# Attention's key and query projections as fp32 products, one head in each half of TensorE's rows, in steps of three token tiles

## The chip, the core and the metric

One NeuronCore of a Trainium2 chip runs the whole program. The metric is device time in microseconds (us) of one execution, the median over runs. PE is TensorE; its weight loads are listed as an engine of their own, PEld. DVE is VectorE, ACT is ScalarE, POOL is GpSimd, and SP issues most of the DMAs.

## What is computed

Linear attention over 4 batches, 8 heads, 576 tokens and a head dimension of 64, then two mixture-of-experts stages over the 2304 tokens. Only the attention is changed:

```python
def phi(x):
    proj = np.einsum('bhsd,df->bhsf', x, w_phi)          # 64 -> 128 features
    proj = proj - np.max(np.abs(proj), axis=-1, keepdims=True)
    return np.concatenate([np.exp(proj), np.exp(-proj)], axis=-1)
q_p, k_p = (phi(q), phi(k))
kv = np.einsum('bhsf,bhsd->bhfd', k_p, v)
z = np.sum(k_p, axis=2)
num = np.einsum('bhsf,bhfd->bhsd', q_p, kv)
den = np.einsum('bhsf,bhf->bhs', q_p, z)[..., None] + 1e-06
return (num / den).astype(np.float32)
```

## The kernel before

Attention runs over eight units; a unit is two batches by two heads, and has nine tiles (j) of 128 tokens with the two heads side by side (64 + 64 columns). For keys and for queries each tile goes through the same chain. A PE transpose (L115, tile `pt`) puts the 128 columns on the partitions, head 0 on rows 0 to 63 and head 1 on rows 64 to 127. ACT copies it out of PSUM rounded to fp32r (`kh`, `qh`, L76), and DVE takes the rounding error (`kl`, `ql`, L79). `proj` (L122) multiplies by a block-diagonal weight that holds `w_phi` twice, rounded (`wbh`) and its error (`wbl`): three fp32r matmuls of 256 columns a tile (L126 to L128) give the features of both heads. `center` (DVE, L133 and L135) subtracts the row's largest absolute value, and `expo` (ACT, L144 and L145) makes exp of both signs, `f`.

From the keys' `f`, `kv_mm` (L180) accumulates the state of both heads over the tiles of a batch. The fifth tile (j = 4) holds 64 tokens of each of the two batches, so its products read rows 0 to 63 for batch 0 and rows 64 to 127 for batch 1. ACT copies the finished state out (`kvt`, L184), `augment` (L193) multiplies it by a constant and ACT copies that to `kvf`. The queries' `f` are transposed (`q_tr`, L212, `ptq`), copied to `fq` (L215), multiplied by `kvf` (`num`, L224, `pn`), copied to `nT` (L225), transposed back (`finish`, L235, `po`) and divided on DVE.

The loop over `g` walks steps of two tiles (one in the last of a unit's five), keys one unit ahead of queries. A step projects its tiles, takes the exponentials of the step before and uses those of the step before that; `fillers` puts `num`, `augment`, `finish` and the next units' transposes between. A scheduler then orders each engine's instructions when the program is built, and each engine runs its own list in that order. After unit 3 the router of the first half of the tokens (`Router.route`) runs on DVE, with a few small matmuls (`pr`, L444 to L453) in PE's list. PSUM has eight banks, which here are two each for the tags T (transposes), Pj (projections), K (the state, one head a bank) and N (the rest). The mixture stages follow, and start while attention ends.

An fp32 product is two matmuls in the trace, with a weight load each, where the program lists one; a transpose and an fp32r product are one.

Of the kernel before, what the change touches and what calls it, by code (L numbers as in the profile page):

```python
# [7 lines left out]
F32 = mybir.dt.float32  # L8
# [30 lines left out]
def attention(tc, nc, cp, q, k, v, w_phi, w_gate, w_skip, lgs, routed, stepped, keys_done, last_steps):  # L39
# [3 lines left out]
    with ExitStack() as ctx:  # L43
# [4 lines left out]
        ps = ctx.enter_context(tc.tile_pool(name="psA", bufs=2, space=PSUM))  # L48

        ident = cp["ident"]  # L50
        ws = c1.tile([P, FH], F32, name="ws")
# [3 lines left out]
        wbh = c1.tile([P, 2 * FH], F32R, name="wbh")  # L55
        wbl = c1.tile([P, 2 * FH], F32R, name="wbl")
        with tc.high_priority():
            for t in (wbh, wbl):
                nc.vector.memset(f32(t), 0.0)
        for h in range(2):  # L60
            w, wh, wl = [t[64 * h : 64 * h + 64] for t in (ws, wbh, wbl)]
            sl = slice(h * FH, h * FH + FH)
            nc.vector.tensor_copy(wh[:, sl], w)
            nc.vector.tensor_tensor(wl[:, sl], w, f32(wh)[:, sl], ALU.subtract)
# [7 lines left out]
        lall = c1.tile([P, NJ, H, 9], F32, name="lall")  # L72

        def split(dst_h, dst_l, src, eng_h="act", lo=None):
            if eng_h == "act":
                nc.scalar.activation(dst_h, src, AF.Copy)  # L76
            else:
                nc.vector.tensor_copy(dst_h, src)
            (lo or nc.vector).tensor_tensor(dst_l, src, f32(dst_h), ALU.subtract)  # L79

        def load_q(bp, hp):
            t = wk.tile([P, NJ, 2, DH], F32, name="qt", tag="qt", bufs=1)
            for b in range(2):
                for h in range(2):
                    (nc.sync if bp or hp else nc.scalar).dma_start(
                        t[64 * b : 64 * b + 64, :, h],
                        q[2 * bp + b, 2 * hp + h].rearrange("(p j) d -> p j d", j=NJ),
                    )
            return t

        def load_kv(src, bp, hp, nm):
            if nm == "vt":
                t = kp.tile([P, NJ, 2, 66], F32, name=nm, tag=nm, bufs=3)
                nc.gpsimd.memset(t[:, :, :, 64:66], 1.0)
            else:
                t = kp.tile([P, NJ, 2, DH], F32, name=nm, tag=nm, bufs=1)
# [10 lines left out]
        def transp(t, nm):  # L107
            pool = kp if nm == "k" else wk
            th = pool.tile([P, NJ, P], F32R, name=nm + "h", tag="Th", bufs=2)
            tl = pool.tile([P, NJ, P], F32R, name=nm + "l", tag="Tl", bufs=2)  # L110

            def group(j0, n):
                pt = ps.tile([P, 4, P], F32, name="pt", tag="T")
                for i in range(n):
                    nc.tensor.transpose(  # L115
                        pt[:, i], t[:, j0 + i].rearrange("p h d -> p (h d)"), ident
                    )
                split(th[:, j0 : j0 + n], tl[:, j0 : j0 + n], pt[:, :n])

            return th, tl, [lambda a=a: group(*a) for a in ((0, 4), (4, 4), (8, 1))]  # L120

        def proj(th, tl, j0, n):  # L122
            pp = ps.tile([P, 2, 2, FH], F32, name="pp", tag="Pj")
            for i in range(n):
# [6 lines left out]
        def center(pp, n):  # L131
            m = wk.tile([P, 2, 2], F32, name="m", tag="m", bufs=4)
            nc.vector.tensor_reduce(m[:, :n], pp[:, :n], AX.X, ALU.max, apply_absolute_value=True)  # L133
            t = wk.tile([P, 2, 2, FH], F32, name="t", tag="t", bufs=2)
            nc.vector.tensor_tensor(  # L135
                t[:, :n], pp[:, :n], m[:, :n].unsqueeze(3).to_broadcast([P, n, 2, FH]), ALU.subtract
            )
            return t

        def expo(t, n, nm):  # L140
            f = (kp if nm == "k" else wk).tile([P, 2, 2, 2, FH], F32, name="f", tag="f", bufs=2)
            tf = t[:, :n].rearrange("p n h f -> p (n h) f")
            ff = f[:, :n].rearrange("p n h s f -> p (n h) s f")
# [4 lines left out]
        units = [(bp, hp) for bp in range(2) for hp in range(4)]  # L148
        QS = ((0, 2), (2, 2), (4, 1), (5, 2), (7, 2))
        KS = ((0, 2), (2, 2), (4, 2), (6, 2), (8, 1))  # L150
        st = {}

        def load(nm, u):
            if u < len(units):
                bp, hp = units[u]
                st[nm, u] = load_q(bp, hp) if nm == "qt" else load_kv(k if nm == "kt" else v, bp, hp, nm)

        def prep_v(u):

            st["v", u] = st.pop(("vt", u))  # L160
            load("vt", u + 1)
            st["kv", u] = wk.tile([P, 2, 2, 2, 74], F32, name="kvf", tag="kvf", bufs=2)

        def kv_mm(u, step):
            vt = st["v", u]
            j0, n = KS[step]
            f = st.pop(("f", u, step))
            for i in range(n):
                j = j0 + i
                for b in (0, 1):  # L170
# [3 lines left out]
                    first, last = (j == 0, j == 4) if b == 0 else (j == 4, j == 8)  # L174
                    for h in range(2):
                        if first:
                            st["acc", h] = ps.tile([65, 256], F32, name="kv", tag="K")
                        acc = st["acc", h]
                        r = f[pr, i, h].rearrange("p s f -> p (s f)")
                        nc.tensor.matmul(acc, vt[pr, j, h, 0:65], r, start=first, stop=last)  # L180
                    if last:
                        kvt = kp.tile([65, 2, 256], F32, name="kvt", tag="kvt")
                        for h in range(2):
# [3 lines left out]
        def augment(u, b):  # L187
            kvt = st.pop(("kvt", u, b))
            hp = units[u][1]
            pa = ps.tile([P, 2, 2, P], F32, name="pa", tag="N")  # L190
# [11 lines left out]
        def q_tr(u, step, f, i):  # L202
            j0, n = QS[step]
            if j0 in (0, 5) and i == 0:
                nj = 5 if j0 == 0 else 4
                st["fq"] = st["fq", u, 0 if j0 == 0 else 5] = wk.tile(
                    [P, 2, 2, 2, nj * 64], F32, name="fq", tag=f"fq{nj}", bufs=2
                )
            pt = ps.tile([P, 4, P], F32, name="ptq", tag="T")
            for h in range(2):  # L210
                for sg in range(2):
                    nc.tensor.transpose(pt[:, 2 * h + sg], f[:, i, h, sg], ident)  # L212
            jj = 64 * ((j0 + i) % 5)
            o = st["fq"][:, :, :, :, jj : jj + 64].rearrange("p h s b t -> p (h s) b t")
            nc.scalar.activation(o, pt.rearrange("p g (b t) -> p g b t", b=2), AF.Copy)  # L215

        def num(u, jc, h, b):
            nj = 5 if jc == 0 else 4
            fq, kvf = st["fq", u, jc], st["kv", u]
            if ("nT", u) not in st:  # L220
                st["nT", u] = wk.tile([74, 2, NJ, 2, 64], F32, name="nT", tag="nT", bufs=1)
# [3 lines left out]
            nc.scalar.activation(  # L225
                st["nT", u][:, h, jc : jc + nj, b], pn.rearrange("f (j t) -> f j t", t=64), AF.Copy
            )

        def finish(u, g):
            bp, hp = units[u]  # L230
            nT = st["nT", u]
            po = ps.tile([P, 2, 3, 74], F32, name="po", tag="N")
            for h in range(2):
                for i in range(3):
                    nc.tensor.transpose(  # L235
                        po[:, h, i], nT[:, h, 3 * g + i].rearrange("f b t -> f (b t)"), ident[0:74, 0:74]
                    )
            rd = wk.tile([P, 2, 3, 1], F32, name="rd", tag="rd", bufs=4)
            nc.vector.tensor_scalar(rd, po[:, :, :, 64:65], 1e-6, None, ALU.add)
            nc.vector.reciprocal(rd, rd)  # L240
            if ("x", bp) not in st:
# [3 lines left out]
                x[:, 3 * g : 3 * g + 3, hp * P : hp * P + P].rearrange("p j (h d) -> p h j d", h=2),  # L245
                po[:, :, :, 0:64],
                rd.to_broadcast([P, 2, 3, 64]),
# [3 lines left out]
                lall[:, 3 * g : 3 * g + 3, 2 * hp : 2 * hp + 2, :].rearrange("p j h e -> p h j e"),  # L251
                po[:, :, :, 65:74],
                rd.to_broadcast([P, 2, 3, 9]),
                ALU.mult,
            )
            if g == 2:
# [4 lines left out]
                routed(bp, x, hp, lg, lambda: ps.tile([P, 512], F32, name="pr", tag="N"))  # L261

        NU = len(units)

        def fillers(u, step):
# [1023 lines left out]
```

## Time and profile before

| | before |
|---|---|
| median of 3 runs (lowest to highest) | 2062.34 us (2060.51 to 2065.01) |
| the profiled execution, and its span | 2056.73 us, 2055.0 us |
| PE busy, of the span | 2017.1 us, 98% |
| DVE, ACT, POOL busy | 62%, 46%, 16% |
| granted clock of PE, mean | 0.998 |

A matmul's end is modelled, and matmuls overlap in the records, so a busy PE may still issue faster or slower: the time that one takes from the next is read from start to start. In a row of the timeline, that is the next PE row's start less this row's start, over the row's count.

### The profile page before, as it was taken

The numbers are of one execution on the slowest core, as the hardware profiler recorded it, in microseconds if no ns is written. First come the engines' busy times: TensorE is split into PE (matmuls) and PEld (weight loads), VectorE is DVE, ScalarE is ACT, GpSimd is POOL, SyncE is SP. The second block draws the span as 40 slices with busy tenths as digits, with TensorE's granted clock in tenths as the row PEclk, the third lists the DMA queues.
The fourth block names the chain that finished last, engine by engine and source line by source line (L and its number), as shares of the span: only waits on it lengthen the run. The fifth ranks groups of instructions, "written<-read, shape, count | busy, mean of one in ns | idle before, by whom it ended". The sixth has DMA issues, their size and how long they took to land.

```text
span 2055.0 us, 29087 instructions
## 1 busy us (share of the span) xinstructions
PE 2017.1 (98%) x10815; PEld 1769.5 (86%) x10815; DVE 1269.2 (62%) x2236; ACT 935.4 (46%) x1885; POOL 337.4 (16%) x271
## 2 busy tenths in 40 slices
PE   8999999998999999999999999999999999999999
PEld 6777778997688998988888899989988898998997
DVE  6456476775586666665745666656565666666563
ACT  5766655554544343343434434434434434444341
POOL 0001032221011122121111221221211212212210
PEclk9999999999999999999999999999999999999999
DMA  6579397665512212213122121121312221212211
GB/s 126 83 102 99 52 238 251 210 209 169 165 42 72 72 52 82 66 58 113 42 72 72 52 82 60 65 83 43 112 42 72 83 66 58 83 52 72 80 54 41
DMA packets 192532, 187.28 MB, mean 91 GB/s; under 512 B 73662, under 2 KB 148158, under 8 KB 192380
## 3 DMA queue, kind: packets, MB, share of 16 engines
q1 hardware_dynamic: 186396, 177.58, 31.6%
q0 software_dynamic: 3456, 7.09, 1.1%
q8 instruction: 87, 1.43, 0.3%
q10 hardware_dynamic: 2528, 0.66, 0.2%
q14 instruction: 65, 0.53, 0.1%
HBM read 163.70 MB, written 23.96 MB: 91 GB/s over the span
## 4 chain that ended last, share of the span: by engine, by line
PE 70%; DMA 2%; DVE 2%; ACT 1%; issue 0%; SPq 0%; ACTq 0%
PE py L1046 36%; PE pb L1010 14%; PE pd L1010 9%; PE pa L1010 9%; DMA r<-in_moe_w_dram 2%; PE pg L887 1%; PE warm L760 1%; ACT w2h L996 0%; SPq L807 0%; DVE wcl L837 0%; DVE w2l L1001 0%; PE pt L879 0%; DMA xr<-x2d 0%; DVE hl L1031 0%; ACT xch L943 0%
## 5 line engine op out<-in xcount | busy, mean ns | idle before, releaser
L1046 PE MATMUL py<-w2l,hh 128*128 128x512 f32 x1152 | 451.5, 392 | 0.0
L1046 PE MATMUL py<-w2h,hh 128*128 128x512 f32 x1152 | 451.3, 392 | 0.1
L1046 PE MATMUL py<-w2h,hl 128*128 128x512 f32 x1152 | 450.3, 391 | 0.0
L1001 DVE TENSOR_TENSOR w2l<-r,w2h 128x512 fp32r<-128x512 f32 x184 | 172.6, 943 | 211.6 <-ACT w2h L996 211.6
L1046 PEld LDWEIGHTS py<-w2l,hh 128*128 128x128 f32 x1152 | 216.1, 188 | 49.1 <-issue 0.6
L1046 PEld LDWEIGHTS py<-w2h,hl 128*128 128x128 f32 x1152 | 216.3, 188 | 37.3
L1046 PEld LDWEIGHTS py<-w2h,hh 128*128 128x128 f32 x1152 | 216.3, 188 | 36.3 <-ACT hh L1026 0.4
L1057 DVE SCALAR_TENSOR_TENSOR acc<-py,lg,acc 128x512 f32<-128x512 f32 x264 | 196.8, 746 | 68.2 <-PE py L1046 67.4
L1026 ACT ACTIVATE hh<-c 128x384 fp32r<-128x384 f32 x192 | 100.9, 525 | 211.9 <-DVE c L1086 117.5
L996 ACT ACTIVATE w2h<-r 128x512 fp32r<-128x512 f32 x184 | 114.7, 624 | 176.1 <-DMA r<-in_moe_w_dram 175.7
L839 POOL TENSOR_TENSOR r<-r,s 128x512 f32<-128x512 f32 x45 | 58.2, 1293 | 657.0 <-DVE wcl L837 645.3
L837 DVE TENSOR_TENSOR wcl<-r,wch 128x512 fp32r<-128x512 f32 x230 | 154.2, 686 | 6.6 <-ACT wch L831 6.5
L1010 PE MATMUL pb<-xch,wch 128*128 128x384 f32 x576 | 149.3, 340 | 8.5 <-ACT v L1018 6.4
L819 POOL TENSOR_TENSOR s<-r 128x512 f32<-128x512 f32 x45 | 57.9, 1288 | 582.4 <-DMA r<-in_moe_w_dram 564.0
L1010 PE MATMUL pb<-xcl,wch 128*128 128x384 f32 x576 | 147.6, 337 | 0.0
L1010 PE MATMUL pb<-xch,wcl 128*128 128x384 f32 x576 | 147.1, 336 | 0.0
L831 ACT ACTIVATE wch<-r 128x512 fp32r<-128x512 f32 x230 | 138.6, 622 | 9.8 <-PE pd L1010 3.0
L1010 PEld LDWEIGHTS pb<-xch,wch 128*128 128x128 f32 x576 | 105.0, 188 | 28.8 <-ACT v L1018 11.0
L1070 DVE TENSOR_TENSOR pb<-pb,s 128x384 f32<-128x384 f32 x96 | 54.3, 566 | 120.8 <-PE pb L1010 64.3
L1018 ACT ACTIVATE s<-pa 128x384 f32<-128x384 f32 x96 | 47.2, 492 | 174.9 <-PE pa L1010 174.9
L1031 DVE SCALAR_TENSOR_TENSOR hl<-c,hh 128x384 fp32r<-128x384 f32 x192 | 106.6, 555 | 6.9 <-ACT hh L1026 6.9
L1018 ACT ACTIVATE z<-pb 128x384 f32<-128x384 f32 x96 | 47.1, 490 | 137.9 <-PE pb L1010 137.8
(250 smaller groups left out, 3882.5 us busy)
## 6 DMA issues: line engine op xcount, KB each, us to landing
r<-in_moe_w_dram SPq DMA_DIRECT2D x168, 512.0 KB, 4.5
r<-in_moe_w_dram SPq DMA_DIRECT2D x184, 256.0 KB, 3.7
xd<-x SPq DMA_DIRECT2D x12, 576.0 KB, 13.0
x2d<-x SPq DMA_DIRECT2D x8, 576.0 KB, 14.4
xr<-x2d SPq DMA_DIRECT2D x18, 256.0 KB, 3.1
out_dram<-acc SPq DMA_DIRECT2D x18, 256.0 KB, 2.0
kt<-in_k_dram SPq DMA_DIRECT2D x32, 128.0 KB, 2.8
vt<-in_v_dram SPq DMA_DIRECT2D x32, 128.0 KB, 3.0
```

What stands on the lines that cost most here:

```text
L819: g.tensor_tensor(s1, a21, a22, ALU.add)
L831: nc.scalar.activation(wc[m, i][0], wsrc[m][i], AF.Copy)
L837: nc.vector.tensor_tensor(l, src[i], f32(h), ALU.subtract)
L839: (nc.gpsimd if m else nc.vector).tensor_tensor(src[3], src[2], src[6], ALU.subtract)
L996: nc.scalar.activation(h, w2r[m, b], AF.Copy)
L1001: nc.vector.tensor_tensor(l, w2r.pop((m, b)), f32(h), ALU.subtract)
L1010: nc.tensor.matmul(dst, w[:, kb, sl], x[:, kb], start=(start and m == 0), stop=(stop and m == 5), skip_group_check=True,)
L1018: nc.scalar.activation(t, src, AF.Copy)
L1026: nc.scalar.activation(hh, src, AF.Relu)
L1031: nc.vector.scalar_tensor_tensor(hl, src, 0.0, f32(hh), ALU.max, ALU.subtract)
L1046: nc.tensor.matmul(py, ht[:, i * P : i * P + P], wt, start=(m == 0), stop=(m == 11))
L1057: nc.vector.scalar_tensor_tensor(accs[t], py, lg[:, t, e : e + 1], accs[t], ALU.mult, ALU.add)
```

## The change

- `proj` multiplies in plain fp32, with no split of the transposed tile or of the weights. For each tile and head, 64 rows of the transposed tile are the weights, 64 rows of `ws` (which has `w_phi` in both halves) stream past, and `tile_position` puts head 0 in the array's rows 0 to 63 and head 1 in rows 64 to 127. Each head writes a PSUM bank of its own. `wbh`, `wbl`, `kl`, `ql` and L79 are gone.
- All steps have three tiles (G = 3), so a unit has three. Transposes go by three tiles, and `num` takes both batches of one head with 192 columns each.
- PSUM: one pool of three banks (tag W) serves `pt`, `ptq`, `pa`, `pn`, `po` and `pr`; the projections have two buffers of two banks; both heads' states share one bank with one buffer, copied out by one ACTIVATE.
- Keys and queries are loaded two units ahead. Some SBUF tiles are padded. The scatters and the splits of the first expert's weights are spread over steps by three.

```diff
-        wbh = c1.tile([P, 2 * FH], F32R, name="wbh")
-        wbl = c1.tile([P, 2 * FH], F32R, name="wbl")
...
-        def split(dst_h, dst_l, src, eng_h="act", lo=None):
-            if eng_h == "act":
-                nc.scalar.activation(dst_h, src, AF.Copy)
...
+        def bank(shape, nm):
+            return ps.tile(shape, F32, name=nm, tag="W", bufs=3)
...
-            pp = ps.tile([P, 2, 2, FH], F32, name="pp", tag="Pj")
-            for i in range(n):
-                o = pp[:, i].rearrange("p h f -> p (h f)")
-                nc.tensor.matmul(o, th[:, j0 + i], wbh, start=True, stop=False)
-                nc.tensor.matmul(o, tl[:, j0 + i], wbh, start=False, stop=False)
-                nc.tensor.matmul(o, th[:, j0 + i], wbl, start=False, stop=True)
+            th = st.pop((nm + "h", w))
+            pp = ps.tile([P, 2, 4, FH], F32, name="pp", tag="Pj", bufs=2)
+            for i in range(G):
+                for h in range(2):
+                    r = slice(64 * h, 64 * h + 64)
+                    nc.tensor.matmul(
+                        pp[:, h, i], th[r, i], ws[r], start=True, stop=True, tile_position=(64 * h, 0)
                     )
             return pp
...
+                    if first:
+                        st["acc"] = ps.tile([65, 2, 256], F32, name="kv", tag="K", bufs=1)
...
                     if last:
                         kvt = kp.tile([65, 2, 256], F32, name="kvt", tag="kvt")
-                        for h in range(2):
-                            nc.scalar.activation(kvt[:, h], st["acc", h], AF.Copy)
+                        nc.scalar.activation(kvt, acc, AF.Copy)
...
-            pn = ps.tile([74, nj * 64], F32, name="pn", tag="N")
-            for fb in range(2):
-                nc.tensor.matmul(pn, kvf[:, b, h, fb], fq[:, h, fb, b], start=(fb == 0), stop=(fb == 1))
+            pn = bank([74, 2, G * 64], "pn")
+            for b in range(2):
+                for fb in range(2):
+                    nc.tensor.matmul(
+                        pn[:, b], kvf[:, b, h, fb], fq[:, h, fb, b], start=(fb == 0), stop=(fb == 1)
+                    )
```

PE's list in the middle of attention, before: one step. In these rows pp is the projection, kh and kl the two parts of the keys, ptq the queries' transposes and kv the state.

```order
L126 MATMUL pp<-wbh,kh 128x256
L127 MATMUL pp<-wbh,kl 128x256
L128 MATMUL pp<-wbl,kh 128x256
L126 MATMUL pp<-wbh,kh 128x256
L127 MATMUL pp<-wbh,kl 128x256
L128 MATMUL pp<-wbl,kh 128x256
L212 MATMUL ptq<-ident,f 128x128 x4
```

PE's list at the like place, now: one step with the end of batch 0's state in it (the single kv row is its last product, the row of four begins with batch 1's first).

```order
L125 MATMUL pp<-ws,kh 128x128 x6
L201 MATMUL ptq<-ident,f 128x128 x3
L125 MATMUL pp<-ws,qh 128x128 x6
L201 MATMUL ptq<-ident,f 128x128 x5
L165 MATMUL kv<-f,vt 65x256
L201 MATMUL ptq<-ident,f 128x128 x4
L165 MATMUL kv<-f,vt 65x256 x4
L213 MATMUL pn<-fq,kvf 74x192 x4
L112 MATMUL pt<-ident,kt 128x128 x3
L213 MATMUL pn<-fq,kvf 74x192 x4
L112 MATMUL pt<-ident,qt 128x128 x3
L227 MATMUL po<-ident,nT 128x74 x6
```

Six projection products (three tiles by two heads) now stand together, between products over all 128 rows; there are 42 such groups in the program, 288 products in all, six groups with keys and queries together. Four transposes stand between the last product of one batch's state and the first of the next.

PE's list behind unit 3's last `po`, now: the router's first matmul, L402, stands here, and reads `ohb`, which DVE makes from that unit's result.

```order
L227 MATMUL po<-ident,nT 128x74 x6
L125 MATMUL pp<-ws,kh 128x128 x6
L165 MATMUL kv<-f,vt 65x256
L125 MATMUL pp<-ws,qh 128x128 x6
L165 MATMUL kv<-f,vt 65x256 x9
L402 LDWEIGHTS upper
L402 MATMUL pr<-ohb,upper 128x72
```

Before, five projections of two tiles, 24 `ptq` transposes and six `kv` products stood between the last `po` and the router's first matmul. On DVE the list from that `po` to `ohb` has two `center` pairs of 768 elements in it now, where it had three and a half of 512.

## Rows read from the trace of the kernel before

**Rows 1.** The page: busy us, and the span in 40 slices.
```profile
PE 2017.1 (98%) x10815; PEld 1769.5 (86%) x10815; DVE 1269.2 (62%) x2236; ACT 935.4 (46%) x1885; POOL 337.4 (16%) x271
...
PE   8999999998999999999999999999999999999999
```

**Rows 2.** Busy time by stage: stretch, its length, then each engine, granted clock, DMA.
```profile
11.00:60.00 49.00, 48.64 (x303) 38.51 (x302) 29.66 (x53) 33.87 (x74) 0.27 (x2) 1.00 0.50 108
60.00:245.00 185.00, 184.44 (x1210) 142.21 (x1209) 101.17 (x256) 127.49 (x274) 11.20 (x14) 1.00 0.66 87
245.00:280.00 35.00, 34.33 (x230) 25.80 (x228) 18.38 (x46) 25.75 (x57) 2.55 (x2) 1.00 1.03 226
```

**Rows 3.** PE's waits that the trace names, 60 to 245 us.
```profile
PE pn L224 <- DVE lall L250: 0.4, 1, 0.4
```

**Rows 4.** PE's timeline: the first 64-row products of three units, one after another.
```profile
75.81 1.07 PE L180 MATMUL kv<-f,vt 64*65 64x256 f32 x4
...
108.83 1.07 PE L180 MATMUL kv<-f,vt 64*65 64x256 f32 x4
...
141.85 1.08 PE L180 MATMUL kv<-f,vt 64*65 64x256 f32 x4
```

**Rows 5.** The timeline of PE: a projection of two tiles, and one of one.
```profile
100.18 0.36 PE L126 MATMUL pp<-wbh,kh 128*128 128x256 f32 x1
100.38 0.28 PE L127 MATMUL pp<-wbh,kl 128*128 128x256 f32 x1
...
100.97 0.60 PE L212 MATMUL ptq<-ident,f 128*128 128x128 f32 x4
...
257.47 0.37 PE L126 MATMUL pp<-wbh,qh 128*128 128x256 f32 x1
...
257.92 0.60 PE L212 MATMUL ptq<-ident,f 128*128 128x128 f32 x4
```

**Rows 6.** The timeline: fp32 products of 128 columns over 65 rows, and what follows.
```profile
258.36 1.06 PE L193 MATMUL pa<-aug,kvt 65*128 65x128 f32 x8
259.25 1.03 PE L224 MATMUL pn<-fq,kvf 128*74 128x256 f32 x4
```

**Rows 7.** The timeline around the fifth tile: 64-row products among 128-row ones.
```profile
109.50 0.81 ACT L184 ACTIVATE kvt<-kv 65x256 f32<-65x256 f32 x2
109.83 0.28 PE L235 MATMUL po<-ident,nT 74*128 74x74 f32 x1
...
110.04 2.08 PE L180 MATMUL kv<-f,vt 64*65 64x256 f32 x8
...
111.96 0.49 PE L235 MATMUL po<-ident,nT 74*128 74x74 f32 x5
```

**Rows 8.** PE's timeline where 64-row products follow a projection, another unit.
```profile
241.47 0.28 PE L128 MATMUL pp<-wbl,qh 128*128 128x256 f32 x1
241.68 1.08 PE L180 MATMUL kv<-f,vt 64*65 64x256 f32 x4
```

**Rows 9.** The timeline: products of 256 columns over 128 rows, and what follows.
```profile
102.55 1.89 PE L180 MATMUL kv<-f,vt 128*65 128x256 f32 x8
...
104.28 1.03 PE L224 MATMUL pn<-fq,kvf 128*74 128x256 f32 x4
```

**Rows 10.** The timeline: weight loads of a projection.
```profile
100.15 0.19 PEld L126 LDWEIGHTS pp<-wbh,kh 128*128 128x128 f32 x1
...
100.26 0.19 PEld L127 LDWEIGHTS pp<-wbh,kl 128*128 128x128 f32 x1
...
100.38 0.19 PEld L128 LDWEIGHTS pp<-wbl,kh 128*128 128x128 f32 x1
```

**Rows 11.** The timeline: an eviction of 512 columns by ACT.
```profile
101.60 0.60 ACT L215 ACTIVATE fq<-ptq 128x512 f32<-128x512 f32 x1 [0.55 <-PE ptq L212]
```

**Rows 12.** The timeline behind unit 3: DVE, then the router's matmul.
```profile
181.68 1.30 DVE L260 TENSOR_REDUCE lg<-lall 128x81 f32<-128x648 f32 x1
...
187.93 0.22 DVE L440 TENSOR_TENSOR ohb<-oh,do 128x72 bf16<-128x72 f32 x1
...
188.58 0.19 PE L444 MATMUL pr<-ohb,upper 128*128 128x72 bf16 x1
```

**Rows 13.** Groups of DVE instructions by line and shape, 60 to 245 us.
```profile
L133 DVE TENSOR_REDUCE m<-pp 128x4 f32<-128x512 f32 x44 | 29.4, 683 | 29.5 <-PE pp L128 29.4
L135 DVE TENSOR_TENSOR t<-pp,m 128x512 f32<-128x512 f32 x44 | 29.3, 685 | 1.2
L79 DVE TENSOR_TENSOR ql<-pt,qh 128x512 fp32r<-128x512 f32 x12 | 8.3, 691 | 39.8 <-ACT qh L76 39.8
```

More of the change, by code (lines that the diff above doesn't have):

```diff
@@ L122, in proj @@
[L122 to L134 removed]
+        units = [(bp, hp) for bp in range(2) for hp in range(4)]
@@ new lines, in attention, with load, transp @@
+        NU = len(units)
+        st = {}
+        def load(nm, u):
+            if u < NU:
+                bp, hp = units[u]
+                st[nm, u] = load_q(bp, hp) if nm == "qt" else load_kv(k if nm == "kt" else v, bp, hp, nm)
+        def transp(nm, w):
+            u, s = divmod(w, NS)
+            if not 0 <= u < NU:
+                return
+            t = st[nm + "t", u]
+            pt = bank([P, G, P], "pt")
+            for i in range(G):
+                nc.tensor.transpose(pt[:, i], t[:, G * s + i].rearrange("p h d -> p (h d)"), ident)
+            th = (kp if nm == "k" else wk).tile([P, G, P], F32, name=nm + "h", tag="th" + nm, bufs=2)
+            nc.scalar.activation(th, pt, AF.Copy)
+            st[nm + "h", w] = th
+            if s == NS - 1:
+                load(nm + "t", u + 2)
@@ L146, in expo, with kv_mm @@
             return f
[L148 to L169, printed above, removed]
+        def kv_mm(w, f):
+            u, s = divmod(w, NS)
+            vt = st["vt", u]
+            if s == 0:
+                st["kv", u] = wk.tile([P, 608], F32, name="kvf", tag="kvf", bufs=2)[:, 0:592].rearrange(
+                    "p (b h s f) -> p b h s f", b=2, h=2, s=2
+                )
+            for i in range(G):
+                j = G * s + i
                 for b in (0, 1):
@@ L174, in kv_mm @@
                     first, last = (j == 0, j == 4) if b == 0 else (j == 4, j == 8)
+                    if first:
+                        st["acc"] = ps.tile([65, 2, 256], F32, name="kv", tag="K", bufs=1)
+                    acc = st["acc"]
                     for h in range(2):
[L176 to L180, printed above, removed]
+                        nc.tensor.matmul(
+                            acc[:, h],
+                            vt[pr, j, h, 0:65],
+                            f[pr, h, i].rearrange("p s f -> p (s f)"),
+                            start=(first and h == 0),
+                            stop=(last and h == 1),
+                            skip_group_check=True,
+                        )
                     if last:
                         kvt = kp.tile([65, 2, 256], F32, name="kvt", tag="kvt")
-                        for h in range(2):
-                            nc.scalar.activation(kvt[:, h], st["acc", h], AF.Copy)
+                        nc.scalar.activation(kvt, acc, AF.Copy)
                         st["kvt", u, b] = kvt
         def augment(u, b):
+            if not 0 <= u < NU:
+                return
             kvt = st.pop(("kvt", u, b))
             hp = units[u][1]
-            pa = ps.tile([P, 2, 2, P], F32, name="pa", tag="N")
+            pa = bank([P, 2, 2, P], "pa")
             for h in range(2):
@@ L200, in augment, with q_tr @@
             nc.scalar.activation(st["kv", u][:, b], pa[:, :, :, 0:74], AF.Copy)
[L202 to L209, printed above, removed]
+        def q_tr(w, f, i):
+            if i == 0:
+                st["fq", w] = wk.tile([P, 2, 2, 2, G * 64], F32, name="fq", tag="fq", bufs=2)
+            pt = bank([P, 4, P], "ptq")
@@ new lines, in attention @@
+        transp("k", 0)
+        for nm in ("kt", "qt", "vt"):
+            load(nm, 1)
+        last = NS * NU - 1
+        t, f, n, d = {}, {}, [], []
+        for g in range(-NS, last + 5):
+            u, s = divmod(g, NS)
+            w = {"k": g + NS, "q": g}
+            ok = {nm: 0 <= w[nm] <= last for nm in w}
+            tn, fn = {}, {}
+            def exps(nm):
+                if nm in t:
+                    fn[nm] = t[nm][0], expo(t[nm][1], nm)
+            tr = [lambda i=i: q_tr(*f["q"], i) for i in range(G)] if "q" in f else []
+            pk = proj("k", w["k"]) if ok["k"] else None
+            pq = proj("q", w["q"]) if ok["q"] else None
@@ L346, in attention @@
-            for c in fillers(u, step):
-                c()
-            pend = new
+            if tr:
+                tr[1]()
+            if ok["q"]:
+                tn["q"] = w["q"], center(pq)
+            if "k" in f:
+                kv_mm(*f["k"])
+            if tr:
+                tr[2]()
+            if n:
+                num(n[0], 0)
+            transp("k", w["k"] + 1)
+            if s == 1:
+                augment(u, 1)
+            if n:
+                num(n[0], 1)
+            transp("q", w["q"] + 1)
@@ L349, in attention @@
+            if d:
+                finish(d[0])
+            if s == 0:
+                augment(u, 0)
+            if s == 2:
+                load("vt", u + 3)
+            d = n
+            n = [f["q"][0]] if "q" in f else []
+            t, f = tn, fn
             stepped()
-            if g == 5 * (NU - 1) + 2:
+            if g == last - 1:
                 kctx.close()
-            if g >= 5 * (NU - 1) + 2 and g < 5 * NU + 3:
+            if last - 1 <= g < last + 3:
                 keys_done()
-            if g == 5 * NU + 3:
+            if g == last + 3:
@@ L642, in transposed @@
             for a in range(2):
-                pt = (ps0 or ps).tile([P, NKB, P], F32, name="pt", tag="T")
+                pt = (ps0.tile([P, NKB, P], F32, name="pt", tag="W", bufs=3) if ps0
+                      else ps.tile([P, NKB, P], F32, name="pt", tag="T"))
                 for kb in range(NKB):
@@ L733, in moe1 @@
             psA = yield
-            for i in range(done, min(8, done + 2) if psA is None else 8):
+            for i in range(done, min(8, done + 3) if psA is None else 8):
                 split_w1(i)
```

164 lines of the change are left out of this document (46 added, 118 removed).

## The prediction

> **What bounds the kernel now.** I read the page first, then stages, then PE's row by row. PE is busy 98% of the span, in nearly every slice [rows 1]. A busy PE need not issue at its best, so the next question is whether it waits in attention: from 11 to 280 us it is busy throughout while DVE and ACT have a quarter or more of their time free [rows 2], and in 185 us the trace names one PE wait of 0.4 us [rows 3]. So attention lasts as long as PE's list takes. Work taken off DVE or ACT there is worth nothing; work taken off PE is worth its whole time, since PE stays full through the stages behind.
>
> A unit comes round every 33.0 us: 108.83 - 75.81, and 141.85 - 108.83 [rows 4]. A projection of two tiles holds PE for 100.97 - 100.18 = 0.79 us, one of a single tile for 257.92 - 257.47 = 0.45 us [rows 5]. A unit has four of two and one of one tile, for keys and again for queries: 8 x 0.79 + 2 x 0.45 = 7.2 us, 57.8 us over eight units. That is what the change replaces. All other PE work keeps its columns, `num` too: 3 x 192 in place of 320 + 256.
>
> **The new projections, priced by rows.** An fp32 product is two passes. The nearest row is L193: fp32, 65 rows, 128 weight columns, 128 columns streamed, eight passes in 259.25 - 258.36 = 0.89 us, 0.111 each [rows 6]. A tile needs four such passes, two in each half of the array. No row has two halves at work at once, so the price lies between four passes in a line (0.444 us a tile) and two (0.222 us).
>
> Products over 64 rows also cost something at their ends. Eight products of 256 columns over 128 rows take 104.28 - 102.55 = 1.73 us, 0.216 each [rows 9]. Four over 64 rows and four over 128 behind them take 111.96 - 110.04 = 1.92 us [rows 7], so 0.19 more, of which the way back to 128 rows is about 0.14 (the four from 108.83 to 109.83 in [rows 4, 7] take 1.00 us for 0.86). Going in costs 241.68 - 241.47 = 0.21 us behind a projection matmul that else gives way after 0.12, so 0.09 [rows 8]; behind a `po`, 110.04 - 109.83 = 0.21 us [rows 7] for an instruction of some 0.06, so 0.15. I take 0.12 in and 0.14 out. The second pass of a group comes 0.20 us behind the first, as in 100.18 to 100.38 [rows 5], because its weights can't be loaded ahead: two loads of 128 columns start 0.11 us apart [rows 10].
>
> If the halves overlap, twelve passes of three tiles stand in seven places (the first alone, five pairs, the last alone). A group takes 0.12 + 0.20 + 6 x 0.111 + 0.14 = 1.13 us. There are 48 projections, 54.2 us; six pairs of groups stand together and save one end each (0.12 + 0.09 + 0.14 = 0.35, together 2.1). That makes 52.1 us, so **-5.7 us** against 57.8. Most of what the overlap gives goes into the ends of the groups.
>
> Why I take the overlapped end: a weight load starts at the very moment at which the matmul before it starts (100.38 in [rows 5] and [rows 10]), so PE runs ahead of its matmuls with loads, and the other half's weights would be ready. The Trainium skill (TensorEngine Tiling (Array Packing), Key Properties) says that different tiles can execute loads and matmuls in parallel; no run here shows it. By it the projections come to the 52.1 us above.
>
> **The rest of the change.**
> - One bank for the state. Before, one head's copy of 0.4 us let the next batch begin [rows 7]. Now one copy of 512 columns (0.60 us [rows 11]) must end first. From the start of the last pass: 0.38 us till its modelled end, 0.60 for the copy, 0.03 for each handover, 1.04 us. PE has its own 0.22 and four transposes (0.44) meanwhile, and idles 0.38. Sixteen such places give 6.1 us; at half of them the way in or out of 64 rows passes in the same time. I take **+3** (0 to 6). Behind PE's waiting `kv` stand `pn`, `pt` and `po`, and so the next step.
> - The router. From unit 3's last `po` to `ohb` DVE needs 1.2 us for the division, 1.3 for L260 [rows 12], two pairs of 768 elements (0.683 and 0.685 us for 512 [rows 13], so 4 x 1.0) and a dozen small ones, about 2: 8.5 us. PE has two groups and ten `kv` products of two passes of 0.216 in that time: 2 x 1.13 + 10 x 0.43 = 6.6 us. L402 then holds up everything behind it: **+2** (0 to 5), once. Before, L444 started 0.43 us after `ohb`, behind work of its own [rows 12].
> - Without L79 [rows 13] the transposed tile is ready 0.7 us sooner: **-1** (-2 to 0), for loads held up here and there. The 48 instructions themselves lie beside PE and give nothing.
> - Three shared banks in place of four for transposes and the rest: each is asked for again three uses later, and the shortest such stretch of PE's list (a `pn`, 1.3 us, and three transposes) exceeds an eviction of 0.60 us [rows 11]. I take 0. If one wait of 0.4 us in each of 24 steps arose, as the one in [rows 3], it would be +10.
> - Loads a unit sooner, padded tiles, scatters by three: beside PE, 0. If the loads crowded the first units' keys, PE would wait there; the DMA engines are busy 0.50 of the time from 11 to 60 us [rows 2], which leaves room.
>
> Sum: -5.7 + 3 + 2 - 1 = -1.7 us. The profiled execution took 2056.73 us for a span of 2055.0; it would take 2055.0 us, and as it lies 5.6 us under the median of the runs shown, the median goes from 2062.34 to **2060.6 us**. About 0.2% (4 us) is what a measurement can tell from no change; this is less.
>
> **Rivals.**
> - *The halves take turns* (slower). Four passes in a line: 144 tiles x 0.444 = 63.9, and 48 x (0.12 + 0.09 + 0.14) - 2.1 = 14.7 for the ends, 78.6 us; +20.8, and with the other terms +25: **2087 us**. One mechanism is enough, and it is the weight load: 0.11 us for 128 columns [rows 10], four a tile. If one load at a time is all that PE does, whatever the half, the loads alone take 0.44 us a tile. The change pays only below (57.8 - 4 - 14.7) / 144 = 0.27 us a tile. For it: in every row loads come one after another. Against: none of those rows has two halves to load. 24%. A variant with three places in place of two, 0.333 us a tile, gives 48.0 + 14.7 + 4 = 66.7, about 2071: 6%.
> - The Trainium skill (TensorE: Matmul & The Clock Gate, What overlaps and what doesn't) says that weight loads overlap a running matmul only where the row groups differ. Then a head's second load would wait for its first pass, 0.11 + 0.11 for each, and the time would be this rival's. The trace disagrees over 128 rows: the load at 100.26 [rows 10] starts during the matmul of 100.18 that ends at 100.54 [rows 5], on the same rows. So I give it no chance of its own beyond the 24%.
> - *The ends are free* (faster). If going in and out costs nothing because PE has to wait at those places anyway, or the second pass comes after 0.11, a group is 0.09 + 7 x 0.111 = 0.87 us, 41.8 in all: -16, and with the other terms about -12, **2050 us**. Against: [rows 7] and [rows 8] show the ends as time with PE idle for nothing else. 22%.
> - *Waits take it* (slower). The shared banks' +10 on top of the forecast: **2070 us**. It decides from 0.25 us a step. Against: ACT has 58 of 185 us free [rows 2]. 8%.
>
> **How the numbers follow.** Forecast 40%, of which 0.15 faster by over 0.2%, 0.21 within, 0.04 slower, as its terms spread by some 5 us; free ends 22% (0.21 faster, 0.01 within); taking turns 24% and the variant 6%, slower; waits 8% (0.01 within, 0.07 slower). Faster 0.36, within 0.23, slower 0.41. The forecast's own range is 2052 to 2067. To hold 8 in 10 it must reach the free ends below and taking turns above: 2046 to 2088.
>
> **What would show it.** The matmuls of L125: if their starts come in pairs a few ns apart at 0.11 us a pair, the halves overlap; if each comes 0.11 us behind the last, they take turns. A group of six products, entry to exit: 1.13 us against 1.5 or more. The first `kv` behind a copied state: 0.4 us of PE idle, released by ACT's copy of the state. L402: PE idle about 2 us behind DVE L398. The unit's period: 33.0 us where nothing changes, 36 if the halves take turns, 31.5 if the ends are free. The prediction is wrong if the stages behind attention change, or if PE in attention is no longer the engine that the others wait for.

## The result, and the profile after

The changed kernel takes **2080.88 us** (median of 5 runs, 2076.36 to 2086.57) beside 2061.26 us for the kernel before on the same chip (5 runs, 2056.59 to 2065.01): a ratio of **1.0095, 95% interval 1.0076 to 1.0114**. It is slower by nearly 1%, 19.6 us. The forecast was no change at 2060.6 us; the time lies inside the stated range, at the end that was meant for another cause.

The profiled execution took 2081.98 us (span 2080.3), 25.3 us of span more than that of before. Behind attention nothing changed: from MoE 1's first matmul to the end it is 1776.2 us, before 1775.6. PE's line of the page, and the span in 40 slices:

```profile
PE 2021.1 (97%) x11087; PEld 1773.7 (85%) x11087; DVE 1250.6 (60%) x2118; ACT 917.5 (44%) x1789; POOL 335.9 (16%) x271
...
PE   7999979998999999999999999999999999999999
```

Attention is the first six slices. The first and the sixth have sevens where [rows 1] has 8 and 9. Busy time by stage, columns as in [rows 2], with two pieces of the tail apart:

```profile
11.00:60.00 49.00, 44.79 (x336) 33.29 (x335) 24.34 (x26) 27.30 (x48) 0.27 (x2) 0.97 0.45 102
60.00:245.00 185.00, 174.09 (x1337) 136.51 (x1336) 81.96 (x175) 108.75 (x198) 11.21 (x14) 1.00 0.63 87
245.00:304.00 59.00, 47.47 (x324) 37.68 (x322) 18.88 (x45) 33.31 (x61) 5.41 (x5) 0.94 0.70 165
...
270.00:280.00 10.00, 3.94 (x38) 3.19 (x36) 3.20 (x8) 5.02 (x10) 2.08 (x2) 0.92 1.13 269
280.00:290.00 10.00, 8.16 (x39) 6.41 (x39) 5.68 (x11) 6.93 (x14) 1.50 (x2) 0.74 1.02 401
```

From 60 to 245 us PE was busy 184.44 us of 185 before [rows 2]; now it is idle for 10.9 us, while DVE works 19 us less and ACT 19 us less. Every engine has less to do and the stage takes longer: something makes them wait for one another. Waits of PE and then of ACT, 60 to 245 us (in total, times, longest):

```profile
PE ptq L201 <- ACT nT L216: 5.0, 11, 0.5
PE pa L186 <- ACT nT L216: 1.8, 4, 0.5
PE kv L165 <- ACT kvt L175: 1.8, 4, 0.8
PE pn L213 <- ACT fq L203: 1.1, 1, 1.1
...
ACT f L143 <- PE pn L213: 12.1, 16, 0.9
```

[Rows 3] had one wait of 0.4 us. The last line is the one to look at: the exponentials f of the queries, which read t (DVE's work), wait sixteen times for a matmul of `num` that has nothing to do with their data. The timeline, PE and ACT: the 64-row products of three units, one step between them, and the tail.

```profile
115.32 2.08 PE L165 MATMUL kv<-f,vt 64*65 64x256 f32 x8
...
133.69 0.84 ACT L143 ACTIVATE f<-t 128x768 f32<-128x768 f32 x1 [0.89 <-PE pn L213]
...
134.30 0.94 PE L125 MATMUL pp<-ws,kh 64*128 64x128 f32 x12
...
134.44 0.83 ACT L144 ACTIVATE f<-t 128x768 f32<-128x768 f32 x1
...
135.18 0.47 ACT L216 ACTIVATE nT<-pn 74x384 f32<-74x384 f32 x1
...
135.70 0.55 PE L201 MATMUL ptq<-ident,f 128*128 128x128 f32 x3 [0.46 <-ACT nT L216]
136.18 0.94 PE L125 MATMUL pp<-ws,qh 64*128 64x128 f32 x12
...
137.05 0.77 PE L201 MATMUL ptq<-ident,f 128*128 128x128 f32 x5
...
149.91 2.08 PE L165 MATMUL kv<-f,vt 64*65 64x256 f32 x8
...
184.49 2.08 PE L165 MATMUL kv<-f,vt 64*65 64x256 f32 x8
...
274.18 1.09 PE L201 MATMUL ptq<-ident,f 128*128 128x128 f32 x8
277.11 1.15 ACT L590 ACTIVATE w1h<-r 128x512 fp32r<-128x512 f32 x2 [4.07 <-issue]
...
279.51 1.55 ACT L203 ACTIVATE fq<-ptq 128x512 f32<-128x512 f32 x3
280.14 5.32 PE L213 MATMUL pn<-fq,kvf 128*74 128x192 f32 x16 [4.87 <-ACT fq L203]
...
289.29 2.82 PE L213 MATMUL pn<-fq,kvf 128*74 128x192 f32 x16 [0.75 <-ACT fq L203]
...
304.09 0.71 PE L627 MATMUL ph<-xTh,w1h 128*128 128x256 f32 x4
```

At 133.69 ACT has stood for 0.89 us until `pn` ended. Its two exponentials then push the copy of `pn` to nT back to 135.18, and PE, which needs that bank of `pn` for the next `ptq`, stands until 135.70. A unit now takes 149.91 - 115.32 = 34.59 us (33.0 in [rows 4]). MoE 1's first matmul, the end of attention, comes at 304.09 us; in the kernel before it came at 279.44. So attention is 24.65 us longer, nearly all of the 25.3.

```profile
279.44 0.74 PE L668 MATMUL ph<-xTh,w1h 128*128 128x256 f32 x4
```

**Why the exponentials wait for num** stands in the diff. `expo` now takes its buffer under the tag `"f" + nm`, which for queries is `"fq"`; `q_tr` takes the tile fq under `tag="fq"`, of the same size in the same pool. So f and fq, which were apart before (`f`, `fq5`, `fq4`), share two buffers. A step's f can't be written until `num` has read the fq that lies there; and by the same rule of the program an fq can't be written until all of the f that lies there is transposed.

### The profile page after: what moved, and what is told of

It reads as the page before. It is cut to its first block, busy times and chain, and to the rows that moved or that the text cites. A ratio compares the mean times of both kernels' runs of the same rounds, so it can differ in the third digit from the quotient of the medians.

```text
span 2080.3 us, 29495 instructions
## 1 busy us (share of the span) xinstructions
PE 2021.1 (97%) x11087; PEld 1773.7 (85%) x11087; DVE 1250.6 (60%) x2118; ACT 917.5 (44%) x1789; POOL 335.9 (16%) x271
## 4 chain that ended last, share of the span: by engine, by line
PE 68%; DMA 3%; DVE 2%; ACT 1%; SPq 1%; issue 0%; ACTq 0%
PE py L1005 35%; PE pb L969 14%; PE pd L969 9%; PE pa L969 8%; DMA r<-in_moe_w_dram 3%; PE pg L846 1%; DVE wcl L796 1%; PE warm L719 1%; SPq L766 1%; ACT w2h L955 0%; DVE hl L990 0%; PE pt L838 0%; DVE c L1057 0%; ACT v L977 0%; DVE w2l L960 0%
## 5 line engine op out<-in xcount | busy, mean ns | idle before, releaser
L960 DVE TENSOR_TENSOR w2l<-r,w2h 128x512 fp32r<-128x512 f32 x184 | 178.9, 979 | 207.9 <-ACT w2h L955 207.9
```

Of the source, the lines that this page charges most:

```text
L960: nc.vector.tensor_tensor(l, w2r.pop((m, b)), f32(h), ALU.subtract)
```

## The experiments

The table gives for each kernel its ratio to the kernel before on the same chip, then from its one profiled execution the time from one unit's second group of 64-row products to the next unit's (the period, as 115.32 to 149.91 above), the same for the unit in which the router runs, and the start of MoE 1's first matmul.

| kernel | ratio, 95% interval | period us | router's unit us | end of attention us |
|---|---|---|---|---|
| before | 1 | 33.03 | 34.29 | 279.44 |
| after | 1.0095 (1.0076 to 1.0114) | 34.59 | 36.75 | 304.09 |
| fq under its own tag | 1.0031 (1.0017 to 1.0045) | 31.82 | 41.98 | 290.64 |
| that, fp32r projection | 1.0049 (1.0033 to 1.0064) | 33.24 | 41.69 | 298.06 |
| own tag, heads in turn | 1.0077 (1.0053 to 1.0101) | 32.80 | 43.44 | 299.99 |
| own tag, later splits | 1.0008 (0.9996 to 1.0019) | 31.81 | 40.30 | 283.72 |
| that, gate's writes apart | 1.0020 (1.0005 to 1.0035) | 31.81 | 44.48 | 288.67 |
| tag shared, three buffers | 0.9991 (0.9980 to 1.0002) | 31.22 | 42.04 | 290.45 |
| that, later splits, x in four | **0.9948** (0.9932 to 0.9965) | 31.23 | 33.59 | 272.97 |
| the last with two buffers | 1.0035 (1.0019 to 1.0050) | 34.59 | 35.74 | 298.75 |
| the last but one, fp32r projection | 1.0009 (0.9992 to 1.0025) | 32.95 | 33.64 | 283.59 |

**A tag of its own.** One line of the kernel after:
```
-  st["fq", w] = wk.tile([P, 2, 2, 2, G * 64], F32, name="fq", tag="fq", bufs=2)
+  st["fq", w] = wk.tile([P, 2, 2, 2, G * 64], F32, name="fq", tag="fqT", bufs=2)
```


> The kernel after with one word changed: the transposed queries fq get a buffer tag of their own (fqT) instead of the tag fq, which the queries' exponentials also carry. Theory A (the two tiles share two buffers, so a step's exponentials of the queries wait until num has read the old fq, and PE then waits for ScalarE): the wait of f at L143 for pn, 13.0 us in 60 to 260 us of the kernel after, goes to under 2 us, PE's waits for fq and nT at L201 and L213 go with it, the unit's period falls from 34.55 us to 33 or below, and the time falls by 15 to 25 us, to about 2056 to 2066. Rival B (three working banks in place of five make PE wait, whatever the tags): the exponentials move earlier, but PE still waits for nT and fq about 25 us, and the time changes by less than 3 us.

Of PE's waits in all of attention, first in after, then in this kernel:

```profile
PE ptq L201 <- ACT nT L216: 7.1, 13, 1.3
...
PE ptq L201 <- ACT nT L216: 0.2, 1, 0.2
```

The period falls by 2.77 us, below that of before, and the exponentials no longer wait for `pn`. The ratio falls by 0.0064, 13 us: less than the 15 to 25 expected, and the profile shows two things in the way: the router's unit is now 10 us longer than its neighbours, and the tail still waits (6.06 us for fq). Rival B, waits from the three banks whatever the tags, falls.

**Three buffers under the shared tag.** The new tag also changed the order of PE's list (the two projections of a step now stand side by side), so the same cause was loosened with the name kept:
```
-  tag="f" + nm, bufs=2)
+  tag="f" + nm, bufs=2 + (nm == "q"))
...
-  name="fq", tag="fq", bufs=2)
+  name="fq", tag="fq", bufs=3)
```


> The kernel after with the tag kept shared between the queries' exponentials and the transposed queries, but with three buffers under it in place of two. Theory A (the wait is for a buffer that the other tile holds): a third buffer takes most of the wait away, the unit's period falls from 34.55 us to between 31.8 and 33, and the time by 8 to 15 us. Rival (it is the name that reorders the list, as the run with the tag of its own also merged the two projections of a step): the period stays above 34 us.

The period falls by 3.37 us, more than expected, and the time by 0.0104 of before, 21.5 us. It is the buffer, not the name. But the third buffer lets the scheduler put the two projections side by side too, so the gain of a unit has two parts. Its window in after, and here:

```profile
115.32:149.91 34.59, 32.78 (x249) 25.67 (x249) 14.13 (x25) 20.48 (x38) 0.13 (x1) 1.00 0.77 103
...
109.61:140.83 31.22, 31.22 (x249) 25.47 (x248) 14.13 (x25) 20.57 (x38) 0.13 (x1) 1.00 0.92 109
```

PE's idle time gives 1.81 of the 3.37 us. The other 1.56 are the same products in a denser list, and no run here takes the two parts apart. The timeline of this kernel shows what is left:

```profile
109.61 2.08 PE L165 MATMUL kv<-f,vt 64*65 64x256 f32 x8
...
140.83 2.09 PE L165 MATMUL kv<-f,vt 64*65 64x256 f32 x8
...
200.93 0.56 DVE L236 TENSOR_TENSOR x<-po,rd 128x384 f32<-128x384 f32 x1 [6.92 <-DMA xd<-gate]
...
269.04 4.42 PE L213 MATMUL pn<-fq,kvf 128*74 128x192 f32 x16 [6.62 <-ACT fq L203]
```

PE runs without a gap from 109.61 to 140.83. Two long waits remain: DVE's of 6.92 us in the router's unit, with PE standing for 5.6 of them, and PE's of 6.62 us in the tail.

**The tail: later splits.** On the kernel with the tag of its own:
```
-        done, psA = 0, None
+        done, psA, more = 0, None, [0, 4, 4]
...
-            for i in range(done, min(8, done + 3) if psA is None else 8):
-                split_w1(i)
+            for i in range(done, min(8, done + more.pop(0)) if psA is None else 8):
+                tc.add_manual_dep(
+                    split_w1(i).ins,
+                    LAST[0].ins.name,
+                    mybir.DependencyInfo(mybir.DependencyClass.NoSync, mybir.DependencyReason.SCHED_ONLY),
+                    reason="behind the step",
+                )
```
LAST is the latest eviction of fq; the dependency only orders ACT's list.


> The run with the tag of its own, and MoE 1's first splits of w1 (ScalarE L590) tied behind the evictions of fq of the two steps that follow the close of the key pool, four and four, in place of three a step from the first. Theory A's second part (in the tail ScalarE stands at a split that waits for its weights, with the evictions of fq behind it, and PE's pn waits 6.06 us at 270.27 us): that wait goes, the last po comes about 5 us earlier than 289.83 us, and the time falls by 3 to 6 us. Rival (the tail lasts as long as its own chain of steps, whatever ScalarE's list holds, or the weights' loads are what the end waits for): the wait moves to a later step and the time changes by less than 2 us.

Attention ends 6.9 us sooner, 1.7 of them in the router's unit, and the ratio falls by 0.0023, 4.8 us, as expected. In the kernel after this is the wait at 280.14: `pn` waits for fq, fq stands in ACT's list behind a split of MoE 1's w1, and the split waits until 277.11 for its weights, whose loads were issued at 264.69 (its row names no releaser; that of the same split in the kernel with the tag of its own, 7.12 us, names the transfer of r). Before, the loads were issued at 250.44, and the first split ran at 263.35 without a wait. Its price is more than 4.87 us: after PE had stood from 275.27 to 280.14 the granted clock is 0.50 from 280.2 to 285.0 us, the lower of the levels 1.2 and 2.4 GHz (the 0.74 above is the mean of ten us), and the sixteen passes take 5.32 us where the next sixteen take 2.82:

```profile
280.20:285.00 4.80, 4.80 (x15) 3.75 (x16) 3.75 (x6) 2.90 (x6) 0.00 (x0) 0.50 1.04 408
```

**The router's unit: the gate's writes taken apart.** On the last kernel, the second of the gate column's two writes goes two steps later, behind an eviction of fq:
```
-            gates.extend([lambda: None, go])
+            gates.extend([lambda: None, lambda: go(slice(0, 1)), lambda: None, lambda: go(slice(1, 2))])
```


> The run with the later splits, and the two writes of the first batch's gate column (1152 packets of 4 bytes each) are taken apart: the one to xd0 stays where it is, the one to xd waits for an eviction of fq two steps later. In the run with the tag of its own the unit in which the router runs lasts 41.99 us where its neighbours last 31.83, and PE waits 2.50, 1.63 and 1.09 us for nothing that the profile shows while the gate's packets fill the DMA engines and loads of instructions land at 193.4 and 197.1 us. If the gate's packets hold the loads of instructions back, the unit falls to 34 to 38 us and the time by 3 to 7 us. If they have nothing to do with it, the unit stays at 41 to 43 us and the time within 2 us of the run with the later splits.

My reason failed: the unit gets longer, 44.48 us, and the time grows by 0.0012 with intervals that overlap. Its timeline shows another wait:

```profile
208.03 0.56 DVE L237 TENSOR_TENSOR x<-po,rd 128x384 f32<-128x384 f32 x1 [10.71 <-DMA qt<-in_q_dram]
...
208.86 1.09 PE L202 MATMUL ptq<-ident,f 128*128 128x128 f32 x4 [8.54 <-DVE lall L243]
```

DVE's first write to the second batch's x stands for 10.71 us. x has one buffer, so the old batch's x must have left through all its transfers. The row names a load of qt, and that of the kernel with three buffers a write of the gate, neither of which is a transfer of x: the releaser is inferred, and that the wait is for x is shown by the next run only. Why the transfers of x, issued by 183.80, take so long is open. Behind DVE stands `po`'s bank, one of the three that `ptq` takes too, so PE stands with it. Before, the same write waited 1.0 us, and PE the 0.4 us of [rows 3]:

```profile
197.57 0.56 DVE L244 TENSOR_TENSOR x<-po,rd 128x384 f32<-128x384 f32 x1 [0.99 <-DMA x2d<-x]
```

In the kernel with the tag of its own this write waits 0.2 us only, though the router's unit is 10 us longer than its neighbours: PE stands there for 2.50 and 1.63 us for nothing that the trace names, and that stays open.

**Both, with x in four tiles.** The kernel with three buffers, with the later splits and:
```
-            if ("x", bp) not in st:
-                st["x", bp] = c1.tile([P, NJ, D], F32, name="x", tag="x", bufs=1)
-            x = st["x", bp]
+            if g == 0:
+                st["x"] = c1.tile([P, NJ, P], F32, name="x", tag=f"x{hp}", bufs=1)
+            x = st["x"]
```
The writes and the transfers then take the tile of their pair of heads; memory stays the same.


> The run with three shared buffers, plus the later splits of w1, plus the attention's result x held as four tiles, one for each pair of heads, in place of one tile for all four. Theory: in the router's unit VectorE's first write to the new batch's x waits until the last transfer out of the old batch's x has landed (10.7 us of idle before L237 in the run with the gate's writes apart, 6.0 us in the run with the later splits), PE stands behind it because po's bank is one of the three that ptq needs too (8.54 and 3.84 us), and tiles of their own take that away; the tail's wait of 6.6 us goes as in the run with the later splits. The router's unit lasts 32 to 34 us, attention ends at 275 to 278 us (before 279.4), and the kernel takes 0.990 to 0.996 of before. Rival (the transfers themselves, or loads of instructions, hold the router's unit up): the unit stays at 39 to 42 us, and the kernel takes 0.996 to 0.999 of before.

The router's unit falls from 42.04 to 33.59 us, DVE's wait at x is gone (the row at 194.14 has none), and the kernel takes **0.9948 of before**: it beats both, and is called the best kernel below. Attention ends 6.5 us before that of the kernel before, and sooner than expected. Its timeline, and its windows from 60 to 245 us:

```profile
127.05 0.94 PE L126 MATMUL pp<-ws,kh 64*128 64x128 f32 x12
127.82 0.84 PE L126 MATMUL pp<-ws,qh 64*128 64x128 f32 x12
128.59 1.09 PE L202 MATMUL ptq<-ident,f 128*128 128x128 f32 x8
...
172.16 2.08 PE L166 MATMUL kv<-f,vt 64*65 64x256 f32 x8
...
194.14 0.56 DVE L237 TENSOR_TENSOR x<-po,rd 128x384 f32<-128x384 f32 x1
...
205.75 2.08 PE L166 MATMUL kv<-f,vt 64*65 64x256 f32 x8
...
272.97 0.71 PE L629 MATMUL ph<-xTh,w1h 128*128 128x256 f32 x4
```
```profile
60.00:245.00 185.00, 183.38 (x1461) 148.91 (x1460) 87.91 (x187) 120.02 (x218) 11.22 (x14) 1.00 0.70 89
```

PE is busy 183.38 of 185 us again, with the change's three banks and its steps of three tiles.

**The same with two buffers.** The last kernel with the change's `bufs=2` in both places.


> The kernel after, its two buffers still shared by exponentials and transposed queries, with the later splits and the four tiles of x alone. Theory A (the shared tag is the main loss): only the tail's wait of 4.9 us goes, the unit's period stays at 34.55 us, and the kernel stays 1.005 to 1.009 of before. Rival (tail and router were the loss, and the steady state would not show in the time): 0.998 to 1.003 of before.

1.0035 lies between the two theories' numbers. The period is 34.59 us as in after. So tail and x together are worth 0.0060 (1.0095 to 1.0035), and the third buffer on top of them 0.0087 (1.0035 to 0.9948), 18 us of time and 25.8 us of attention, denser list included. The shared buffers are the largest part of the loss, not all of it.

**The same with the fp32r projection.** The kernel that beats both, with before's three products a tile, block-diagonal weights and VectorE's low parts in place of L126's passes.


> The first of these three, with the projection undone: three fp32r products of each tile with the block-diagonal weights and VectorE's subtractions, as in before. If the row halves' saving reaches the time once the waits are gone, it is 9 to 13 us slower than the first (the steady period was 1.40 us a unit longer in the pair of runs with the tag of its own, 11 us over eight units). If other engines or MoE 1's loads take the saving back, it is within 4 us of it.

12.5 us slower by the medians (2070.98 and 2058.52 us), 10.6 us of attention. The saving of the row halves reaches the time. The pair of projections in its timeline, against 127.05 to 128.59 above:

```profile
131.83 0.37 PE L139 MATMUL pp<-wbh,kh 128*128 128x256 f32 x1
...
134.06 1.04 PE L215 MATMUL ptq<-ident,f 128*128 128x128 f32 x8
```

Six tiles take 2.23 us there, and 1.54 us by row halves. The earlier pair, both with the tag of its own and the waits of router and tail, moved the same way in the period (33.24 and 31.82):


> As the run with the tag of its own, but with the projection of the kernel before: three fp32r products of each tile with the block-diagonal weights, and VectorE's subtractions for the low parts. Steps of three tiles, the loop order and the bank plan stay those of after. Theory A (the row halves overlap and PE's projection fell from 57.8 to about 47 us): 10 to 13 us slower than the run with the tag of its own, more where VectorE's subtractions delay a product. Rival C (with the tag mended, ScalarE or the banks set the pace and the projection's price is hidden): within 4 us of it.

Its time moved by 0.0018, 3.7 us, which is the rival's number and which the intervals don't separate from nothing. The saving shows in full in the pair without those waits.

**Heads in turn.** The kernel with the tag of its own, the loops of `proj` exchanged:
```
-            for i in range(G):
-                for h in range(2):
+            for h in range(2):
+                for i in range(G):
```


> As the run with the tag of its own, but the six products of a step are issued head 0's three and then head 1's three, so that neighbours of the list use the same row half. If two halves run together only because neighbours alternate between them, a group of six takes 12 passes of 0.11 us in place of 6 pairs, 0.66 us more for each of 48 groups, and the kernel is 20 to 32 us slower than the run with the tag of its own. If the halves are served from queues of their own, whatever the order, or other engines set the pace, it is within 4 us.

Neither: 0.0046 slower, 9.5 us, and 0.98 us a unit, 0.16 for each of its six groups where 0.66 would be full turns. The timeline:

```profile
139.91 1.26 PE L125 MATMUL pp<-ws,kh 64*128 64x128 f32 x12
141.02 1.26 PE L125 MATMUL pp<-ws,qh 64*128 64x128 f32 x12
142.22 0.33 PE L201 MATMUL ptq<-ident,f 128*128 128x128 f32 x1
```

A group takes 1.11 to 1.20 us here, longer than 0.87 and shorter than twelve places at 0.11 and its ends. So part of head 1's passes still run beside head 0's: in the first of these groups three pairs of passes start within 6 ns. In the unit's other two steps the two groups overlap as well, and take 1.86 and 1.93 us together where they took 1.54 and 1.60.

## Why the prediction was wrong, step by step

**The premise.** "So attention lasts as long as PE's list takes" is the step that failed. It held of the kernel before, and I carried it over by pricing PE's list alone; PE's idle time in attention grew from 4.5 to 29.0 us. I looked for new waits only at PSUM ("Three shared banks ... I take 0"), and didn't compare which tiles share an SBUF buffer before and after, though the two tags stand in the diff. The same banks serve the kernel at 0.9948 with 1.6 us of waits at `ptq` from 11 to 273 us, so the banks' 0 was nearly right; the buffers' price was 25.8 us of attention, 15.6 of them idle time of PE. "Waits take it" had the right kind, 8% and +10 us, at the wrong place. "The halves take turns" gave 2087 us, near the result, by a mechanism that isn't there.

**The list itself** was mis-sized too. Attention in parts, from each matmul's start to the next one's, less the idle time that the trace shows before the next:

| kernel | projections us | rest of PE's list us | PE idle us |
|---|---|---|---|
| before | 63.1 | 205.6 | 4.5 |
| after | 44.1 | 226.0 | 29.0 |
| two buffers, later splits, x in four | 43.8 | 224.0 | 24.9 |
| the best kernel | 39.5 | 218.3 | 9.3 |
| the best kernel, fp32r projection | 57.0 | 213.7 | 7.3 |

"All other PE work keeps its columns" put at nothing a term that measures 20 us in after and 13 us in the best kernel; the transposes `ptq` alone take 7.6 and 3.8 us more. It eats the whole saving of 19 us on the projections in after: the list as it stands there takes 270.0 us without its idle time, some 2.5 of them at the lower clock in the tail, and before's 268.7. Before's projections took 63.1 us where I had 57.8, as not all of them stand in pairs like the one of [rows 5].

**The overlap** was right, and mis-sized. What starts within 12 ns of 134.30 us in the kernel after:

```profile
134.30 0.19 PEld L125 LDWEIGHTS pp<-ws,kh 64*128 64x128 f32 x2
134.30 0.38 PE L125 MATMUL pp<-ws,kh 64*128 64x128 f32 x2
```

Two loads and two products, one of each half. This is what the Trainium skill (TensorEngine Tiling (Array Packing), Key Properties) says of tiles, loads and matmuls in parallel; the trace agrees. A group takes 137.05 - 136.18 = 0.87 us, where I had 1.13, and two groups together 1.54 where I had 1.91. The passes stand in six places, not seven, as the first two start together as well. The second pair comes 0.21 us behind the first, as I had it; the next instruction comes 0.21 behind the last pair, so 0.10 for the way out where I had 0.14; the way in falls into the row before and isn't in this count. That 0.87 is also what the rival of free ends had is luck: its seven places and a second pass after 0.11 are not in the trace. Against before's products in the same steps the row halves are worth 12.5 us, where I had 5.7 against steps of two tiles.

**One bank for the state**, +3: PE's waits for kvt at `kv` are 1.8 us from 60 to 245 us in after and 1.4 us in all of attention in the best kernel.

**The router**, +2: at L402 PE waits under 0.4 us in attention of the best kernel. The router's unit exceeds its neighbours by 2.2 us in after and by 1.3 in before, so the change itself added 0.9. The place that counts is x, which I hadn't named: where the trace shows DVE's wait of 6 to 11 us at x, the unit exceeds its neighbours by 8 to 13 us; with x in four tiles by 0.7 to 2.4.

**Left out altogether:** the tail. The step on moved work should have asked where the splits of w1 stand in ACT's list when the pool closes in steps of three tiles; they stood ahead of fq, for weights issued later than before. **Loads a unit sooner**, 0: PE's first transposes wait 2.6 us for kt in after, once; nothing was tried on it. The **-1** for L79's absence was not tried by itself.

**What stays open.** The kernels with the tag of its own and with three buffers end attention at the same time (290.64 and 290.45 us) and differ by 0.0040 in time: from MoE 1's first matmul to the end their profiled executions take 1787.7 and 1778.2 us, and no run here says why. In the best kernel's it is 1793.9 us, where before has 1775.6; that execution, of 2068.64 us, is the slowest of ten, with the median at 2058.52, so ends of attention and ratios don't come from the same executions. One part is known: MoE 1's gather has become a wait, which before had 1.6 us:

```profile
PE pt L606 <- DMA xg<-xd,ix: 5.6, 1, 5.6
```

## What to carry to other kernels

When a change renames or regroups tiles, list which tiles share a buffer before and after, and ask of each write what must have read the buffer last; a wait of an engine for an instruction that doesn't feed it can be the mark of a shared buffer. A saving on the bounding engine is worth its price only while that engine stays the bound, so price first the waits that the change can add on the others, then the saving, and read from rows what a new order costs the work that keeps its columns. When a stage becomes faster, look again at single buffers and at whatever stands in an engine's list waiting for a transfer: x in one tile was there before, and cost 1.0 us of DVE until the work reached it sooner.

## What the runs showed of the hardware

Passes in the two row halves start together, weight loads included: two of each within 12 ns. Six pairs take 0.77 us where two groups adjoin (127.05 to 127.82), 0.13 each (the second pair comes 0.21 us behind the first, the others 0.11), where a single pass has 0.11 [rows 6]: the second half is nearly free. Nor must neighbours in the list alternate between the halves: with three products of one head ahead of the other's, two groups take 1.86 to 2.31 us, more than 1.54 and less than twenty-four places at 0.11.

In the tail of after PE stood for 4.87 us, and the granted clock fell: 0.50 (1.2 GHz) from 280.2 to 285.0 us, where `pn`'s sixteen passes took 5.32 us in place of 2.82. This wait in PE's list cost half as much again as it lasted.
